# Score products in groups of four PSUM banks, a finer list schedule, and four smaller reorderings in an attention, expert and MLP kernel

## The chip, the cores and the metric

The kernel runs on one core of a Trainium2 chip. The metric is the device time of one execution in microseconds (us), smaller is better; a kernel's time is the median of several executions. The engines are PE (matrix products), DVE and ACT (elementwise work and copies out of PSUM), POOL (indirect gathers and scatters, some copies) and SP, whose queue issues most of the DMAs. PSUM has eight banks; PE writes its products there, and DVE and ACT read them out.

## The reference

Three layers in a row, in float32.

```
# 1 attention with mixing of the 12 heads before and after the softmax; q, k, v: 4 x 12 x 448 x 64
s = scale * q @ k^T;   s = einsum('bhij,hg->bgij', s, w_pre)
p = exp(s - max s);    p = p / (sum p + 1e-9)
p = einsum('bhij,hg->bgij', p, w_post);   x = p @ v        # then 1792 tokens x 768
# 2 one expert of 8 per token, chosen by argmax of x @ w_gate, weighted by its softmax
y = gate * (relu(x @ w1[e]) @ w2[e])                       # 768 -> 1024 -> 768
# 3 MLP
h = y @ w_in;  g = h * cos(h);  out = g @ w_out            # 768 -> 2048 -> 768
```

## The kernel before

**Products in three parts.** Most products are float32 split into a high and a low part (ACT makes the high part by a cast, DVE the low part by a subtraction), and three of the four partial products are added up in PSUM: high x high, high x low, low x high.

**Attention.** The work is 16 chunks: each of the 4 batches has three of 120 query rows and one of 88. For a chunk, `qk(X, j)` makes the scores of heads 2j and 2j+1 in two banks by six matmuls that use half of the array's rows each (the planner calls this tiling "row"). `brought` copies them to SBUF (tile S). A DMA from S to a tile x (`relay`) regroups them into blocks of up to 10 rows with their 12 heads on the partitions; there are 9 or 12 blocks to a chunk, 180 in all. A block is premixed (PE, m, line 515), reduced and exponentiated (DVE nm, ACT E), and mixed again (PE, pa, line 536) into AT. `products` multiplies a chunk's AT by v (PE, px, tiling "col"), and `gates` makes the router's logits of a few chunks.

**First batch.** The scores of chunk 0 are made by an order written out by hand, under `manual_schedule`: k and q of batch 0 arrive in pieces (`load_first`), POOL copies each pair of heads side by side (`beside`), PE transposes them (tp), ACT and DVE split them (KH, KL, QH, QL), and PE makes scores. `spin(n)` issues n products into a bank that nobody reads. `repeat` is a small product with w_pre and w_post; the mixing matrices `kpre` and `kpost` are made of its result by `mixers` at the end of this part.

**List schedule.** All other attention work is issued in an order that `Plan.run` finds when the program is built. Work is given as generators of steps; each step has a price per engine (time held, time until the result is there), PSUM banks and buffers to take and give back, and events to wait for. `Plan.run` takes the step that can start soonest, and among those within 0.02 us the one with the lowest rank, where a change of PE's tiling is charged `TURN` = 0.19 us and `LOYAL` is added to its rank. A DMA is a step on SP that holds SP 0.8 us and lands after a set time, whatever else is in flight. `score(X, j)` covers two calls of `qk` (four heads) as two steps of two banks each. `Banks` hands the planned banks to the tiles; outside the plan it takes the eight banks in turn. The plan begins where the first batch's part ends, with estimates of when each engine and bank is free; there every bank counts as free at time 0, from bank 0 on.

**From attention to the experts.** `between` runs the last chunk's products and logits among the first expert slot's first layer. `Routing.slots` makes the slot table, `slots_mm` turns it into row numbers (a product pid, then a copy to `ids` on DVE), and `Experts.lead` runs slot 0's second layer: `hT` transposes the hidden values and splits them (hh, hl), `product2` multiplies, and the token rows of slot 1 are gathered by POOL (`gather(1)`) after the first of the eight steps of `product2` and transposed (`xT(1)`, px, line 1174) after the sixth.

**MLP.** Four chunks of tokens (`CHUNKS`, 2, 4, 4 and 4 tiles of 128). `part2` adds, for each of 16 slices f of the hidden layer and each token tile, gh x oh, gh x ol and gl x oh into two banks: 512 columns in one, 256 in half of another. After f = 15 ACT copies the 512 columns, DVE the 256, and POOL scatters the rows to the output.

## Time and profile before

| | |
|---|---|
| median of 3 executions | 1329.72 us (1328.36 to 1333.59) |
| the profiled execution | 1326.42 us; span of its instructions 1324.7 us |
| busy share of the span | PE 98%, PE's weight loads 82%, DVE 79%, ACT 62%, POOL 5% |
| instructions | 24862 |
| attention, of that its first batch by hand | 0 to about 501 us, 0 to about 20 us |
| experts, with the way there from attention | about 501 to 843 us |
| MLP | about 833 us to the end (a little overlap) |

A row of a timeline gives start, duration, engine, source line, operation, the tiles written and read, and how many instructions were merged; in brackets stands the idle time of the engine before it and what ended it. A matmul's end is modelled and overlaps the next one's start, so distances between starts tell PE's pace better than durations do.

### The profile page before, as it was taken

The numbers are of one execution on the slowest core, as the hardware profiler recorded it, in microseconds if no ns is written. First come the engines' busy times: TensorE is split into PE (matmuls) and PEld (weight loads), VectorE is DVE, ScalarE is ACT, GpSimd is POOL, SyncE is SP. The second block draws the span as 40 slices with busy tenths as digits, with TensorE's granted clock in tenths as the row PEclk, the third lists the DMA queues.
The fourth block names the chain that finished last, engine by engine and source line by source line (L and its number), as shares of the span: only waits on it lengthen the run. The fifth ranks groups of instructions, "written<-read, shape, count | busy, mean of one in ns | idle before, by whom it ended". The sixth has DMA issues, their size and how long they took to land.

```text
span 1324.7 us, 24862 instructions
## 1 busy us (share of the span) xinstructions
PE 1300.1 (98%) x8855; PEld 1083.7 (82%) x8855; DVE 1042.6 (79%) x2410; ACT 824.0 (62%) x1509; POOL 67.8 (5%) x84
## 2 busy tenths in 40 slices
PE   8899999999999998999999999999999999999997
PEld 5677777677777777899999999998888888888886
DVE  7687888788778889899999999897666666666663
ACT  6566666566666657888889888765444444444432
POOL 3000000000000000100010000011000000001001
PEclk9999999999999999999999999999999999999999
DMA  6758757675757547278545772464433343224201
GB/s 162 229 192 228 228 169 223 203 235 172 218 188 220 175 153 247 87 270 319 185 167 190 286 266 93 147 225 168 152 101 115 108 132 109 85 96 142 94 25 48
DMA packets 146368, 227.02 MB, mean 171 GB/s; under 512 B 44800, under 2 KB 108480, under 8 KB 146240
## 3 DMA queue, kind: packets, MB, share of 16 engines
q1 hardware_dynamic: 139904, 200.20, 46.9%
q0 software_dynamic: 3744, 18.09, 4.0%
q10 hardware_dynamic: 2592, 7.08, 1.4%
q8 instruction: 73, 1.20, 0.4%
q14 instruction: 55, 0.45, 0.1%
HBM read 217.87 MB, written 31.85 MB: 189 GB/s over the span
## 4 chain that ended last, share of the span: by engine, by line
PE 59%; DVE 0%; ACT 0%; POOLq 0%; issue 0%
PE op L1466 18%; PE dh L1522 17%; PE yp L1280 11%; PE h L1246 11%; PE ph L1267 1%; PE px L1174 1%; PE dpt L1403 1%; POOLq L1769 0%; ACT dhs L1526 0%; ACT r L1489 0%; PE gspg L1023 0%; DVE r L1486 0%; DVE r L1487 0%; DVE o L1474 0%; PE pc L1059 0%
## 5 line engine op out<-in xcount | busy, mean ns | idle before, releaser
L1086 DVE TENSOR_TENSOR wl<-r,wh 128x768 fp32r<-128x768 f32 (+1 forms) x246 | 249.1, 1061 | 11.2 <-ACT wh L1085 8.3
L1085 ACT CAST wh<-r 128x768 fp32r<-128x768 f32 (+1 forms) x246 | 224.2, 931 | 37.9 <-PE h L1246 31.1
L536 PEld LDWEIGHTS pa<-kr,E 120*112 120x112 f32 (+1 forms) x1440 | 166.5, 177 | 45.6 <-issue 31.4
L536 PE MATMUL pa<-kr,E 120*112 120x120 f32 (+1 forms) x1440 | 180.7, 269 | 0.8 <-DVE kr L530 0.4
L1086 DVE TENSOR_TENSOR wil<-wi,wih 128x768 fp32r<-128x768 f32 x64 | 60.9, 953 | 131.3 <-ACT wih L1085 131.3
L515 PE MATMUL m<-x,kpre 120*120 120x448 f32 x360 | 159.8, 548 | 3.9 <-DMA x<-S 3.8
L522 ACT ACTIVATE E<-m,nm 120x448 f32<-120x448 f32 x180 | 114.5, 636 | 57.9 <-DVE nm L518 31.5
L1085 ACT CAST wih<-wi 128x768 fp32r<-128x768 f32 x64 | 53.9, 844 | 155.0 <-PE dh L1522 154.0
L518 DVE TENSOR_REDUCE nm<-m 120x1 f32<-120x448 f32 x180 | 111.2, 619 | 26.5 <-PE m L515 22.0
L1466 PE MATMUL op<-woh,gl 128*128 128x512 f32 x448 | 116.8, 341 | 0.0
L1466 PE MATMUL op<-woh,gh 128*128 128x512 f32 x448 | 116.0, 339 | 0.0
L1466 PE MATMUL op<-wol,gh 128*128 128x512 f32 x448 | 115.3, 338 | 0.0
L1522 PE MATMUL dh<-dxh,wih 128*128 128x512 f32 (+1 forms) x384 | 111.2, 364 | 0.1
L1522 PE MATMUL dh<-dxl,wih 128*128 128x512 f32 (+1 forms) x384 | 110.7, 363 | 0.0
L1522 PE MATMUL dh<-dxh,wil 128*128 128x512 f32 (+1 forms) x384 | 109.9, 363 | 0.0
L539 ACT COPY AT<-pa 112x480 f32<-112x480 f32 (+1 forms) x111 | 63.1, 568 | 43.8 <-PE pa L536 41.3
L1085 ACT CAST woh<-wo 128x768 fp32r<-128x768 f32 x64 | 53.4, 836 | 55.2 <-PE op L1466 54.6
L347 PEld LDWEIGHTS px<-AT,vn 112*64 112x64 f32 x1536 | 73.7, 137 | 10.2 <-issue 4.6
L1466 PEld LDWEIGHTS op<-woh,gh 128*128 128x128 f32 x448 | 70.7, 189 | 11.1 <-DVE o L1474 0.3
L1522 PEld LDWEIGHTS dh<-dxl,wih 128*128 128x128 f32 x384 | 70.1, 189 | 11.5
L1522 PEld LDWEIGHTS dh<-dxh,wil 128*128 128x128 f32 x384 | 69.8, 189 | 11.3
L515 PEld LDWEIGHTS m<-x,kpre 120*120 120x120 f32 x360 | 55.1, 183 | 28.9 <-issue 18.2
(290 smaller groups left out, 2561.1 us busy)
## 6 DMA issues: line engine op xcount, KB each, us to landing
r<-in_moe_w_dram SPq DMA_DIRECT2D x54, 1024.0 KB
r<-in_moe_w_dram SPq DMA_DIRECT2D x72, 768.0 KB
x<-S SPq DMA_DIRECT2D x172, 210.0 KB
wi<-wi SPq DMA_DIRECT2D x32, 768.0 KB
wo<-wo SPq DMA_DIRECT2D x32, 768.0 KB
W<-in_moe_w_in_dram SPq DMA_DIRECT2D x32, 384.0 KB
W<-in_moe_w_out_dram SPq DMA_DIRECT2D x32, 384.0 KB
ys<-y ACTq DMA_DIRECT2D x17, 384.0 KB
```

The source lines that it names most:

```text
L347: nc.tensor.matmul(px[64 * e : 64 * e + 64, pr, :n], VN[b, g // 3][:, g % 3, cc], AT[X][:, cc, g, :n], start=(cc == 0), stop=(cc == 3))
L515: nc.tensor.matmul(ps[:M, :S], kpre[:M, :M], x[:M], start=True, stop=True)
L518: nc.vector.reduce_max(nm[:M], ps[:M, :S], axis=AX.X, negate=True)
L522: last["act"] = nc.scalar.activation(e[:M], ps[:M, :S], AF.Exp, bias=nm[:M], scale=1.0, accum_out=sg[:M])
L536: nc.tensor.matmul(pa[:112, c, :120], e[:M, c * 112 : c * 112 + 112], kr[:M], start=True, stop=True)
L539: last["post"] = by[eng](AT[X][:, :, :, j0 : j0 + m], pa[:112, :, :120].rearrange("p c (g i) -> p c g i", i=10)[:, :, :, :m])
L1085: self.latest["A"] = nc.scalar.copy(hi, src).ins
L1086: self.latest["V"] = nc.vector.tensor_tensor(lo, src, hi.bitcast(F32), op=ALU.subtract).ins
L1246: self.nc.tensor.matmul(hp[n], a[:, k], w[:, n * 512 : n * 512 + 512], start=(k == 0 and i == 0), stop=(k == 5 and i == 2))
L1280: self.nc.tensor.matmul(yp[n][:, :384], a[:, k], w[:, n * 384 : n * 384 + 384], start=(k == 0 and i == 0), stop=(k == 7 and i == 2))
L1466: nc.tensor.matmul(bank[:, to], g[:, t * P : t * P + P], w[:, of], start=first, stop=(f == 15 and i == 2), skip_group_check=(n == 1))
L1522: nc.tensor.matmul(hp[:, :N], w[:, k], x[:, k, :N], start=(k == 0 and i == 0), stop=(k == 5 and i == 2))
```

## The change

It has these parts:

- `score` becomes one step for two calls of `qk`: it takes four banks at once, and its twelve matmuls follow each other. Scores get an earlier rank (n0 - 6 for n0 - 4), and `LOYAL` is 3 for 2.
- DMA steps carry what SP is held (0.34 to 1.36 us, by kind) and their size; the plan keeps a clock of the wire (260 KB per us) that all transfers share, and adds 0.6 us ahead and 1.97 us behind.
- The plan's starting state has its own times for each engine, bank and event. `Banks` keeps the banks in the order of their last use, and the plan starts from that order.
- First batch: the pieces of heads 4 to 7 are cut in two (two more DMAs each way are issued: one for k, one for q), `repeat` moves from the second to the fifth round, and two spins follow the second round's scores.
- `between`: the cast and subtraction of weight piece 4 (`ex.first(4)`) move behind the last chunk's logits and their copy.
- `lead`: `slots_mm` and `gather(1)` move from behind the first step of `product2` to between `hT`'s transposes and its splits.
- `part2`: the three 512-column products of a tile come first, then the three of 256 columns.

```diff
@@ -50,10 +50,13 @@
 
 
     def __init__(self, pool, n):
-        self.pool, self.given, self.turns = pool, [], itertools.cycle(range(n))
+        self.pool, self.given, self.turns = pool, [], list(range(n))
 
     def tile(self, shape, dt, tag, name):
-        i = self.given.pop(0) if self.given else next(self.turns)
+        i = self.given.pop(0) if self.given else self.turns[0]
+        if i in self.turns:
+            self.turns.remove(i)
+            self.turns.append(i)
         return self.pool.tile(shape, dt, tag=f"{tag}{i}", name=name)
 
 
@@ -66,12 +69,13 @@
 
 
 
-    HOP, TURN, STAY, LOYAL, DRIFT = 0.06, 0.19, 0.02, 2.0, 0.0
+    LEAD, LAND, RATE = 0.6, 1.97, 260.0
+    HOP, TURN, STAY, LOYAL, DRIFT = 0.06, 0.19, 0.02, 3, 0.0
 
     def __init__(self, slots, banks=None, seed=0):
         self.free = {t: [(0.0, i) for i in range(n)] for t, n in slots.items()}
         self.at, self.engine, self.pending, self.held = {}, {}, [], {}
-        self.now = self.reached = 0.0
+        self.now = self.reached = self.wire = 0.0
         self.tiling, self.banks, self.luck = "full", banks, random.Random(seed)
 
     def add(self, rank, task, bg=False):
@@ -141,6 +145,9 @@
             self.now = start
             self.engine[e] = start + hold
             end = start + lat
+            if "kb" in step:
+                self.wire = max(self.wire, start + hold + self.LEAD) + step["kb"] / self.RATE
+                end = self.wire + self.LAND
             for a in step.get("give", ()):
                 tag, key = (a, id(task)) if isinstance(a, str) else a
                 s = self.held[tag, key if tag == "q" else 0].pop(0)
@@ -150,8 +157,7 @@
                 self.at[ev] = end
             self.go(rank, task, bg, start + hold if step.get("onward") else end + self.HOP, e, slots)
         if self.banks:
-            self.banks.given = []
-            self.banks.turns = itertools.cycle([s for t, s in self.free["q"]])
+            self.banks.given, self.banks.turns = [], [s for t, s in self.free["q"]]
 
 
 class Taken:
@@ -244,7 +250,7 @@
     def load_first(a, src, h0, h1, cs=slice(0, 4)):
         nc.sync.dma_start(out=a[:, h0:h1, cs], in_=src[0, h0:h1].rearrange("h (p c) d -> p h c d", c=4)[:, :, cs])
 
-    for h0, h1 in ((0, 2), (2, 4), (4, 8), (8, H)):
+    for h0, h1 in ((0, 2), (2, 4), (4, 6), (6, 8), (8, H)):
         load_first(fk, k, h0, h1)
         load_first(fq, q, h0, h1, slice(0, 2))
     load_first(fq, q, 0, 6, slice(2, 4))
@@ -465,10 +471,12 @@
                 pk, pq_ = turned(0, j, 0), turned(0, j, 1, first)
                 if j == 0:
                     spin(2)
-                if j == 1:
+                if j == 4:
                     repeat()
                 if j > 0:
                     ps = qk(0, j - 1)
+                if j == 1:
+                    spin(2)
                 split_k(0, j, pk)
                 split_q(0, j, pq_, first)
             else:
@@ -501,13 +509,13 @@
         return {"ACT": (0.05 + n * 0.00092, 0.12 + n * 0.00092), "DVE": (n * 0.00124, 0.07 + n * 0.00124)}
 
     def dma(d):
-        return {"SP": (0.8, d)}
+        return {"SP": (d, d)}
 
     plan = Plan({"q": 8, "x": 6, "E": 4, "kr": 4, "Sb": 1, "AT": 1, "W": 2, "sq": 2, "f": 2, "kn": 2, "qn": 2, "xr": 1, "xc": 4, "vn": 0}, pq, 0)
 
     def block(n):
         X, be, rs, m, M = geom(n)
-        yield dict(run=dma(4.2), take=["x"], on=[("S", X, h) for h in range(H)], ends=[("x", n)])
+        yield dict(run=dma(0.86), kb=18 * M // 10, take=["x"], on=[("S", X, h) for h in range(H)], ends=[("x", n)])
         relay(n)
         yield dict(run=pe(0.752), take=["q"], reached=n)
         x = XR.pop(n)
@@ -547,8 +555,9 @@
             on += [("x", k) for k in range(first_of[X - 2], end_of[X - 2] + 1)]
         if j:
             on.append(("s", X, j - 1))
-        for i in (j, j + 1):
-            yield dict(run=pe(0.61), tiling="row", onward=True, take=[("q", ("s", X, i, h)) for h in range(2)], on=on, ends=[("s", X, i)])
+        js = range(j, j + 2)
+        yield dict(run=pe(0.6 * len(js) + 0.01), tiling="row", take=[("q", ("s", X, i, h)) for i in js for h in range(2)], on=on, ends=[("s", X, i) for i in js])
+        for i in js:
             SC[X, i] = qk(X, i)
 
     def brought(X, j, i):
@@ -559,7 +568,7 @@
     def heads(b, j, s_):
 
         tag, src, t = (("kn", k, KN), ("qn", q, QN))[s_]
-        yield dict(run=dma(4.0), take=[tag])
+        yield dict(run=dma(1.36), kb=230, take=[tag])
         load_pair(b, j, sk.tile([112, 4, 2, D], F32, tag=tag, name=f"{tag}{b}_{j}", bufs=2), src, t)
         yield dict(run=pe(0.385), take=["q"], on=[("s", 4 * b - 1, j)])
         ps = turned(b, j, s_)
@@ -574,7 +583,7 @@
 
     def values(b):
         for g in range(4):
-            yield dict(run=dma(3.5), on=[("av", 4 * b - 1, 0), ("av", 4 * b - 1, 1)] if b else [("x", 3)], ends=[("V", b)] if g == 3 else [])
+            yield dict(run=dma(0.58), kb=344, on=[("av", 4 * b - 1, 0), ("av", 4 * b - 1, 1)] if b else [("x", 3)], ends=[("V", b)] if g == 3 else [])
             load_v(b, g)
 
     def products(X):
@@ -636,29 +645,31 @@
         yield dict(run={"none": (0.0, 0.0)}, on=[("xcs", G_[-1])], give=["xc"])
 
     def piece(i, load, square, bits, store):
-        yield dict(run=dma(6.0), take=["W"])
+        yield dict(run=dma(0.58), kb=393, take=["W"])
         load(i)
         yield dict(run=act(0.56), take=["sq"])
         square(i)
         for d, op in zip((0.36, 0.56, 0.56), bits(i)):
             yield dict(run=dve(d), take=["f"] if d == 0.36 else [], give=["W", "sq"] if False else [])
             op()
-        yield dict(run=dma(3.5), give=["W", "sq"])
+        yield dict(run=dma(0.42), kb=197, give=["W", "sq"])
         store(i)
         yield dict(run={"none": (0.0, 0.0)}, give=["f"])
 
     for h in range(H):
-        plan.at["S", 0, h] = 0.0
+        plan.at["S", 0, h] = 0.7
     for j in range(H // 2):
-        plan.at["K", 0, j] = plan.at["Q", 0, j] = 0.0
+        plan.at["K", 0, j] = 0.0
+        plan.at["Q", 0, j] = 1.4 + 0.4 * j
+    plan.free["q"] = [(max(0.0, 0.6 + 0.4 * (i - 1)) if i > 1 else 0.0, s) for i, s in enumerate(pq.turns)]
     plan.add(4, values(0))
-    plan.engine.update(ACT=1.0, DVE=1.0, PE=0.5, SP=0.0)
+    plan.engine.update(ACT=3.0, DVE=3.3, PE=2.2, SP=0.0)
     for n in range(N):
         plan.add(n, block(n))
     for X in range(1, len(chunks)):
         n0, nb0 = first_of[X], CH[chunks[X - 1][1]][2]
         for j in range(H // 2):
-            r = n0 - 4 - 8 * (X % 4 == 3) - (H - 2 - 2 * j) * (nb0 - 5) / H
+            r = n0 - 6 - 8 * (X % 4 == 3) - (H - 2 - 2 * j) * (nb0 - 5) / H
             if j % 2 == 0:
                 plan.add(r, score(X, j))
             for i in range(2):
@@ -1094,7 +1105,7 @@
             yield
 
 
-MID, XT1 = 1, 6
+XT1 = 6
 
 ORDER = [(0, 0), (0, 1), (1, 0), (1, 1), (2, 0), (2, 1)]
 
@@ -1257,14 +1268,19 @@
         self.X.pop(s)
         return self.relu(hp, self.wk.tile([P, 1024], F32, tag="hr", name=f"hr{s}", bufs=1))
 
-    def hT(self, s, hr):
+    def hT(self, s, hr, mid=None):
         nc, wk = self.nc, self.wk
         hh = wk.tile([P, 8, P], F32R, tag="hh", name=f"hh{s}", bufs=1)
         hl = wk.tile([P, 8, P], F32R, tag="hl", name=f"hl{s}", bufs=1)
+        ps = []
         for half in range(2):
             p = self.pt.tile([P, 512], F32, tag="t", name=f"ph{s}_{half}")
             for j in range(4):
                 nc.tensor.transpose(p[:, j * P : j * P + P], hr[:, (4 * half + j) * P : (4 * half + j + 1) * P], self.ident)
+            ps.append(p)
+        if mid:
+            mid()
+        for half, p in enumerate(ps):
             pv = p.rearrange("p (a t) -> p a t", a=4)
             k = slice(4 * half, 4 * half + 4)
             self.spw.latest["A"] = nc.scalar.copy(hh[:, k], pv).ins
@@ -1315,12 +1331,13 @@
 
     def lead(self, mid):
 
-        self.hT(0, self.hr0)
+        def slots():
+            self.ids = mid()
+            self.gather(1)
+
+        self.hT(0, self.hr0, slots)
         yp = self.yp0 = self.hidden2(0)
-        self.product2(0, range(MID), yp)
-        self.ids = mid()
-        self.gather(1)
-        self.product2(0, range(MID, XT1), yp)
+        self.product2(0, range(XT1), yp)
         for _ in range(XT1, 8):
             self.split()
         self.xT(1)
@@ -1459,8 +1476,8 @@
             ci, f, gh, gl, oh, ol, op = item
             t0, nt = CH[ci]
             for t in tiles or range(nt):
-                for i, (g, w) in enumerate(((gh, oh), (gh, ol), (gl, oh))):
-                    for n, (bank, to, of) in enumerate(spans(op, t)):
+                for n, (bank, to, of) in enumerate(spans(op, t)):
+                    for i, (g, w) in enumerate(((gh, oh), (gh, ol), (gl, oh))):
 
                         first = f == 0 and i == 0 and (n == 0 or t % 2 == 0)
                         nc.tensor.matmul(
@@ -1618,9 +1635,9 @@
         ex.product1(0, 0, hp)
         ex.early_parts()
         att.av_out(X, 1, px, A)
-        ex.first(4)
         pl = att.logits_mm((X,))
         att.logits_out((X,), pl, V)
+        ex.first(4)
         att.rows_out(X, 0, att.rows_mm(X, 0), A)
         att.logit_tiles(X)
         ro.last(ctx, att.pq, "q")

```

## Rows read from the trace of the kernel before

**Rows 1.** Stretches: window, length, busy us of PE, PEld, DVE, ACT, POOL, PEclk, DMA share, GB/s

```profile
30.00:60.00 30.00, 26.14 (x212) 18.76 (x212) 20.27 (x69) 17.12 (x42) 0.00 (x0) 1.00 0.86 255
60.00:120.00 60.00, 58.68 (x483) 44.91 (x480) 49.60 (x144) 40.21 (x98) 0.00 (x0) 1.00 0.66 198
```

**Rows 2.** Chain that ended last: start us, us, what; MLP

```profile
863.12 4.32 PE dh L1522 x36
...
881.60 4.51 PE dh L1522 x36
...
1159.27 8.19 PE dh L1522 x36
1167.45 8.47 PE op L1466 x48
```

**Rows 3.** Timeline of the first batch, one wait

```profile
9.04 0.35 PE L437 MATMUL wps<-wpp,rep 12*120 12x24 f32 x2 [1.12 <-DMA wpp<-in_w_post_dram]
```

**Rows 4.** Stretches of 2 us in the first batch

```profile
8.00:10.00 2.00, 0.96 (x8) 0.74 (x8) 0.57 (x2) 0.43 (x2) 0.87 (x2) 1.00 1.13 238
10.00:12.00 2.00, 2.00 (x15) 1.17 (x13) 0.78 (x3) 1.65 (x4) 1.35 (x4) 0.80 1.18 227
12.00:14.00 2.00, 2.00 (x12) 1.67 (x12) 1.54 (x4) 1.31 (x3) 1.61 (x4) 0.50 1.13 198
14.00:16.00 2.00, 2.00 (x16) 1.17 (x14) 0.49 (x2) 1.23 (x3) 1.89 (x6) 0.85 0.17 22
```

**Rows 5.** Timeline where the list schedule begins

```profile
19.86 1.88 DVE L235 TENSOR_TENSOR QL<-tp,QH 128x224 fp32r<-128x224 f32 x6 [0.15 <-ACT QH L234]
...
21.79 0.47 PE L284 MATMUL s<-KH,QH 64*120 64x448 f32 x2 [1.48 <-DVE QL L235]
...
25.53 1.47 SPq L194 DMA_DIRECT2D kn<-in_k_dram  x2
...
35.60 1.01 PE L515 MATMUL m<-x,kpre 120*120 120x448 f32 x2 [1.96 <-DMA x<-S]
```

**Rows 6.** Waits from 30 to 495 us: who waited for what, total us, times, longest

```profile
PE m L515 <- DMA x<-S: 3.8, 6, 2.0
PE tp L216 <- DMA kn<-in_k_dram: 3.6, 4, 1.2
```

**Rows 7.** Timeline of PE at one visit to the scores

```profile
61.11 0.37 PE L284 MATMUL s<-KL,QH 64*120 64x448 f32 x2
61.32 0.37 PE L284 MATMUL s<-KH,QL 64*120 64x448 f32 x2
61.62 1.07 PE L536 MATMUL pa<-kr,E 120*112 120x120 f32 x8
```

**Rows 8.** Group of one line, 25 to 500 us: busy us, mean ns, idle before

```profile
L557 ACT COPY S<-s 120x448 f32<-120x448 f32 (+1 forms) x115 | 56.0, 538 | 12.5 <-PE s L284 11.6
```

**Rows 9.** Timeline between attention and experts

```profile
506.38 3.48 DVE L1235 TENSOR_TENSOR wl<-r,wh 128x1024 fp32r<-128x1024 f32 x3
...
509.78 0.23 DVE L358 COPY LT<-pl 8x88 f32<-8x88 f32 x1
```

**Rows 10.** Timeline of slot 0's second layer

```profile
519.70 1.28 DVE L1271 TENSOR_TENSOR hl<-ph,hh 128x512 fp32r<-128x512 f32 x2
...
521.76 0.17 DVE L951 CAST ids<-pid 128x21 int32<-128x21 f32 x1
...
522.21 3.19 POOL L1166 DMA_INDIRECT xg<-xs,ids  x1 [36.20 <-DMA r<-in_moe_w_dram]
...
528.26 0.87 PE L1174 MATMUL px<-ident,xg 128*128 128x128 f32 x6 [1.84 <-DMA xg<-xs,ids]
...
529.36 1.02 DVE L1184 TENSOR_TENSOR xl<-px,xh 128x384 fp32r<-128x384 f32 x2 [0.28 <-ACT xh L1180]
```

**Rows 11.** Timeline of the end

```profile
1317.53 0.59 ACT L1473 COPY o<-op 128x512 f32<-128x512 f32 x1 [1.62 <-PE op L1466]
...
1318.84 0.97 POOL L1475 DMA_INDIRECT out_dram<-o,cout  x1 [0.79 <-ACT o L1473]
```

## The prediction, made before the changed kernel was run

> **What bounds the kernel now.** I read the stretches first: PE is busy in almost all of every later stretch, and between 30 and 60 us it falls behind: 26.1 of 30 us, against 58.7 of 60 just after [rows 1]. Then the chain that ended last: from the expert stage on it is PE products back to back, 8.19 us for 36 products of 512 columns, 8.47 us for 48 of 512 and 256 alternating [rows 2]. DVE and ACT are off that chain. So time can be won in three ways only: take waits of PE away, give PE fewer or cheaper products, or shorten the tail. The third reading was of PE's waits, and they sit in five places: the first batch, where PE waits and its clock drops [rows 3, 4]; the start of the list schedule [rows 5]; waits for regrouped scores (x) and for the next batch's k in attention [rows 6]; the hand-over to the experts [rows 9, 10]; and the end [rows 11]. The sum is made against the profiled execution, 1326.42 us (span 1324.7, so 1.7 us lie around it). That is 3.3 us under the median of the runs, 1329.72; I take the saving as the same and carry it to the median.
>
> **First batch: -1.8 us.** PE waits 1.12 us for w_post before the small product of `repeat`, with the first scores queued behind it [rows 3]. In the fifth round that matrix has long landed, so the move costs only the product (0.35 us), and its copy on DVE no longer holds up the splits behind it. PE was busy 0.96 of 2 us from 8 to 10, and then the granted clock is 0.80, 0.50 and 0.85 in the next three stretches, the lower level for part of them [rows 4]. PE was called busy all that time, so the price of the drop is 2 x (0.20 + 0.50 + 0.15) = 1.7 us of work done at half speed. The two spins go into PE's queue ahead of the third round's transposes; they hold PE some 0.6 us, hidden by the wait for that pair's pieces, which the smaller pieces shorten; uncovered they cost that 0.6. The two extra DMAs take SP about 0.5 us each, while the DMA engines are the limit up to 14 us (share 1.13 to 1.18) and free after it (0.17) [rows 4], so they delay nothing that sets the end. Bounds: if ACT's and POOL's copies set the pace, 0.5; if wait and clock both go, 1.12 + 1.7 = 2.8. I take 1.8, between, since ACT is busy 1.65 of 2 us in one of these stretches.
>
> **Start of the plan: -1.2 us.** The first planned scores start at 21.79, after a wait of 1.48 us for a QL [rows 5]. They need the first head pair's QL alone, ready some 0.3 us into the six (19.86 to 21.74). They wait for the last: the plan gives bank 0, and counting tiles through the first batch bank 0 is the last one used (33 tiles, eight banks). With banks in order of use the four-bank step needs two score copies and the first two QL, about 20.5 to 20.6. Bounds 0 (x then sets the start) to 1.48; I take 1.2.
>
> **DMA prices: -2.5 and -1.8 us.** The plan holds SP 0.8 us for a pair's k where the trace shows 1.47 us for its two issues [rows 5], so real transfers of x fall ever further behind the planned ones; PE then waits 1.96 us for one at 35.60. In all PE waits 3.8 us for x in six places, and 3.6 us for k in four places, at the batch changes [rows 6]. With held times and a shared wire in the plan these steps stand later in PE's order, and blocks of ready work fill in. The list remains greedy: it still issues k, v or weight pieces whenever SP is free. Bounds 0 and 3.8, and 0 and 3.6. I take two thirds of the first, whose cause is seen, and half of the second.
>
> **Visits to the scores: -0.7, and +1.0 for the banks.** A visit costs a change of tiling twice: from the last score product to the next postmix 0.30 us, where score products follow each other at 0.21 [rows 7], so 0.09, and by the estimate of the same on the way in, about 0.19 a visit. I counted 49 visits in PE's timeline, 27 of a single pair; 45 four-head steps allow at most 45, and where steps follow each other fewer. Saved: 4 x 0.19 = 0.8 at the least expected, less if LOYAL's merging of whole runs of steps is lost; 0.7. Against it stands the added wait. Four of eight banks must be free together; behind a waiting step stand the premixes and postmixes, on PE in order. One bank comes free with one copy, 0.54 us on ACT [rows 8]. If the plan's prices are right it places the step where the banks are free; I price it at 0.54 us in two places, +1.0. From both sides: 0, or 0.54 at each of 45 steps, 24 us (a rival below).
> A page speaks against this part: the Trainium skill, TensorEngine Tiling (Array Packing), Gotcha 1: PSUM Pressure, says that row tiling raises the pressure on PSUM, as each row tile needs a bank of its own. By that rule the price would lie nearer the upper bound; the trace does not contradict it, as DVE and ACT do have waits for scores but PE's listed waits are on DMAs.
>
> **Hand-over to the experts: -0.2 and -1.8 us.** The copy LT (0.23 us, at 509.78) stands on DVE right behind three weight subtractions of 1.16 us [rows 9]. The move puts one of them behind it, so PE gets the logits' transposes, and the first layer behind them, up to 1.1 us sooner; but the copy of the transposed logits then waits behind that subtraction, and DVE is nearly full here. Bounds 0 and 1.1; I take 0.2.
> The gather of slot 1 starts at 522.21, right after `ids` at 521.76, and PE waits 1.84 us for it at 528.26 [rows 10]; this puts 6.05 us from start to use, a span that I keep. After the change two small products stand ahead of the splits hl on PE, and `ids` ahead of hl on DVE: it can run when hl now starts, at 519.70, instead of 521.76, 2.06 us sooner; hl and the first products behind it slip by about 0.2. Nothing else is on POOL's queue, and the gather is moved past no load of SP's. PE's wait shrinks to nearly nothing, 1.84 - 0.05 = 1.8. What comes next is xl, which DVE ends at 530.38; slot 1's first layer begins at about 532.4 and needs xl only at its third product, so there is cover of about 2 us, and it is just used up. Bounds 1.0 to 2.0.
>
> **Wide products first: -1.5 us.** A 512 and a 256 in turn take 8.47/24 = 353 ns. Wide ones alone take 8.19/36 = 227.5, narrow ones alone 4.32/36 = 120 or 4.51/36 = 125 [rows 2]: 347.5 to 353. So mixing costs 0.4 to 5.4 ns a pair. There are 14 x 16 x 3 = 672 pairs; if the cost sits at the changes of width, the new order keeps one in three, and saves 448 x (0.4 to 5.4) = 0.2 to 2.4 us. I take 1.5, nearer the quieter stretch of narrow ones. gl is needed 0.25 us sooner in each tile; its maker runs a slice ahead, so this is free.
> The Trainium skill, TensorE: Matmul & The Clock Gate, section Wait — 56ns, not 53.3ns?, has each matmul cost its columns plus a fixed amount; then the order makes nothing, and this term is 0. The rows neither prove nor exclude it, as 125 gives nearly that.
>
> **Tail: -0.3 us.** ACT's copy of the last 512 columns takes 0.59 us, and the last scatter starts 0.7 us after it ends [rows 11]. Its bank is now complete three narrow products (0.37 us) sooner; DVE's copy, which is shorter, then decides. Bounds 0.1 and 0.37.
>
> **Sum.** -1.8 - 1.2 - 2.5 - 1.8 - 0.7 + 1.0 - 0.2 - 1.8 - 1.5 - 0.3 = -10.8 us: 1326.42 - 10.8 = 1315.6 for a profiled execution, 1329.72 - 10.8 = 1318.9, say 1319, as a median.
>
> **Rivals.**
> 1. The plan gives back what it wins: another greedy order has other waits, in other places, and the plan's four terms (-1.2 of the start excepted) come to 0. They are -2.5 - 1.8 - 0.7 + 1.0 = -4.0, so 1323. For it: the waits of rows 6 are few and scattered and any new order draws new ones. Against: the price of SP is off by a factor that the trace shows.
> 2. Slower: four banks at once are not free where the plan believes so. At 0.54 us for each of 45 steps the change costs 24 us in place of 1.0, 1319 + 23 = 1342. It decides for slower (above 1336.4) from 18.4/45 = 0.4 us a step. For it: copies of scores end late where DVE and ACT wait for PE [rows 8] and the page above. Against: PE's waits on banks are absent among the large ones of the trace before.
> 3. All DMA waits and the clock's drop go: 1.0 more in the first batch, 1.3 on x, 1.8 on k, 1.0 on banks, together 5.1: 1314; more, if the visits merge as well.
> 4. The order of the widths makes nothing, as the page has it: the forecast moves to 1320.5. It goes beside any of the others; I give it 4 in 10.
>
> **How the numbers follow.** Forecast 0.50, rival 1 0.25, rival 3 0.15, rival 2 0.10. A measurement tells about 0.5% from no change, 6.65 us: faster is below 1323.1, slower above 1336.4. Of the forecast nearly all (0.47) is faster, of rival 1 half (0.12), of rival 3 all: 0.74. Rival 2 gives slower 0.08 and 0.02 between. Same: 0.18. The range reaches from 1310 (every bound of waits at its better end) to 1327 (rival 1 with the low bounds of first batch and hand-over, 1329.72 - 2.7); outside are most of rival 2 and a little of both ends.
>
> **What would show it.** Right: the granted clock stays at 1.00 in the first 20 us; the first planned score starts under 0.5 us after the last transposes; waits of m for x and of tp for k halve; 45 visits or fewer; px of slot 1 starts without a wait, 2 us closer to hl; 48 products of `part2` take 8.40 us or less. Wrong: new waits of PE's weight loads on copies of S or AT around the scores, a first batch that ends no sooner because POOL's copies or landings set it, or a stall of DVE in slot 0's second layer that takes the gather's gain.

## The result, and the profile after

| | median us | lowest to highest, runs | ratio to before, 95% interval |
|---|---|---|---|
| before | 1329.53 | 1328.36 to 1333.85, 6 | |
| changed | 1314.22 | 1313.68 to 1316.48, 6 | 0.9891 [0.9874, 0.9908] |

The change makes the kernel 1.1% faster: by the ratio 14.5 us, between 12.2 and 16.8. The profiled execution took 1316.38 us (span 1314.5) for 1326.42 (1324.7), a difference of only 10.2: that of before lay 3.1 us under its median, that of after 2.2 over its own. The 10.2 us come from these stretches, each taken between two starts that both traces have:

| stretch | before | after | difference |
|---|---|---|---|
| start to first premix (m) | 25.59 | 23.76 | -1.83 |
| first m to last postmix (pa) | 475.23 | 468.75 | -6.48 |
| last pa to slot 0's second layer (yp) | 18.48 | 17.69 | -0.79 |
| first yp to slot 3's first layer | 41.42 | 41.97 | +0.55 |
| slot 3 to the MLP's first dh | 272.09 | 272.09 | 0 |
| first dh to the end of the last op | 484.80 | 483.13 | -1.67 |
| from there to the end | 7.1 | 7.1 | 0 |

**Attention.** The stretches of the changed kernel, in the columns of [rows 1], with one row for nearly all of the list schedule:

```profile
30.00:60.00 30.00, 27.50 (x196) 18.73 (x197) 22.87 (x71) 17.40 (x42) 0.00 (x0) 1.00 0.84 228
60.00:120.00 60.00, 60.00 (x528) 46.79 (x526) 51.06 (x152) 41.06 (x101) 0.00 (x0) 1.00 0.75 217
24.00:490.00 466.00, 460.82 (x4193) 352.81 (x4193) 384.75 (x1298) 291.24 (x714) 1.31 (x2) 1.00 0.69 205
```

The last row in the trace of before:

```profile
24.00:490.00 466.00, 457.25 (x4142) 346.73 (x4139) 375.54 (x1269) 294.77 (x717) 1.23 (x2) 1.00 0.66 204
```

PE is idle 5.18 of these 466 us, where it was 8.75, and does 51 more products in them. The waits of PE from 30 to 495 us in the changed kernel, as in [rows 6]:

```profile
PE m L523 <- DMA x<-S: 2.3, 5, 0.9
PE tp L222 <- DMA qn<-in_q_dram: 1.0, 1, 1.0
```

The waits for x fell from 3.8 to 2.3 us, those for k from 3.6 to none that is listed; one for q came in. The timeline of PE at a visit to the scores shows the grouped step: a switch still costs 0.30 us where the products follow each other at 0.20 to 0.21, as in [rows 7], but there are 42 visits for 49, and 40 of them take two pairs.

```profile
67.90 0.37 PE L290 MATMUL s<-KL,QH 64*88 64x448 f32 x2
68.11 0.37 PE L290 MATMUL s<-KH,QL 64*88 64x448 f32 x2
68.41 1.07 PE L544 MATMUL pa<-kr,E 120*112 120x120 f32 x8
```

**First batch and the plan's start.** Stretches of 2 us, as in [rows 4], then the timeline, as in [rows 5]:

```profile
8.00:10.00 2.00, 2.00 (x20) 1.28 (x16) 0.98 (x3) 1.80 (x5) 1.15 (x3) 1.00 1.14 245
10.00:12.00 2.00, 2.00 (x18) 1.25 (x15) 1.93 (x4) 1.59 (x5) 0.61 (x1) 1.00 1.19 224
12.00:14.00 2.00, 1.91 (x15) 1.19 (x14) 1.14 (x5) 1.54 (x4) 1.81 (x5) 1.00 1.10 181
14.00:16.00 2.00, 2.00 (x18) 1.34 (x16) 1.64 (x5) 1.74 (x4) 1.66 (x5) 1.00 0.05 9
```

```profile
17.43 1.88 DVE L241 TENSOR_TENSOR QL<-tp,QH 128x224 fp32r<-128x224 f32 x6 [0.15 <-ACT QH L240]
...
17.77 1.42 SPq L200 DMA_DIRECT2D kn<-in_k_dram  x2
17.82 0.47 PE L290 MATMUL s<-KH,QH 64*120 64x448 f32 x2
...
19.30 5.13 SPq L307 DMA_DIRECT2D x<-S  x6
...
23.76 1.50 PE L523 MATMUL m<-x,kpre 120*120 120x448 f32 x3 [2.08 <-DMA x<-S]
```

PE is busy in all but 0.09 us from 8 to 16 us and its granted clock stays at 1.00, the 2.4 GHz level, where it had been busy for 0.96 of the 2 us from 8 to 10 and the clock fell. The splits QL start 2.4 us sooner than in [rows 5], and the first planned scores start 0.4 us after the first of them, without a wait. But two loads of k now stand on SP's queue ahead of the first x, which is issued 1.5 us later than it could be, and PE waits 2.08 us for it.

**Hand-over.** The timeline, as in [rows 10]; SPq is SP's queue of DMAs, and L1699 the line of a branch of the program that all engines pass:

```profile
510.43 0.17 DVE L962 CAST ids<-pid 128x21 int32<-128x21 f32 x1
510.52 1.28 DVE L1287 TENSOR_TENSOR hl<-ph,hh 128x512 fp32r<-128x512 f32 x2
510.88 0.98 POOL L1177 DMA_INDIRECT xg<-xs,ids  x1 [38.82 <-DVE ids L962]
...
515.29 0.07 SPq L1165 DMA_DIRECT2D r<-in_moe_w_dram  x1
...
516.91 0.82 PE L1185 MATMUL px<-ident,xg 128*128 128x128 f32 x6
...
524.84 6.74 ACT L1096 CAST wh<-r 128x1024 fp32r<-128x1024 f32 x7 [4.50 <-SPq L1699]
525.45 7.47 SPq L1161 DMA_DIRECT2D r<-in_moe_w_dram  x5
...
532.12 1.14 PE L1279 MATMUL ph<-ident,hr 128*128 128x128 f32 x8 [1.67 <-ACT hr L1261]
```

The wait for the gather is gone, and slot 1's first layer starts 10.82 us after the first yp (521.02 - 510.20) for 13.12 before. Then ACT stands still for 4.50 us at the branch, the relu hr of slot 1 comes late behind its casts, and PE waits 1.67 us for it. Slot 3 starts no sooner after the first yp than before (41.97 us for 41.42).

**MLP and tail.** Pieces of the chain that ended last, as in [rows 2], and the last copies and scatter, as in [rows 11]:

```profile
854.48 4.32 PE dh L1539 x36
...
1265.79 8.18 PE dh L1539 x36
1273.97 8.38 PE op L1483 x48
```

```profile
1307.09 0.59 ACT L1490 COPY o<-op 128x512 f32<-128x512 f32 x1 [1.60 <-PE op L1483]
1307.43 0.42 DVE L1491 COPY o<-op 128x256 f32<-128x256 f32 x1 [1.76 <-PE op L1483]
1308.63 0.97 POOL L1492 DMA_INDIRECT out_dram<-o,cout  x1 [0.77 <-issue]
```

48 products take 8.38 us for 8.47. At the end ACT's copy now starts before DVE's, but DVE's copy of the narrow columns is as late as it was, and the last scatter starts 1.24 us after the last product (1.23 before).

### The profile page after: what moved, and what is told of

Read it like the earlier page. It is cut to its first block, busy times and chain, and to the rows that moved or that the text cites. A ratio compares the mean times of both kernels' runs of the same rounds, so it can differ in the third digit from the quotient of the medians.

```text
span 1314.5 us, 24861 instructions
## 1 busy us (share of the span) xinstructions
PE 1294.2 (98%) x8857; PEld 1083.5 (82%) x8857; DVE 1046.8 (80%) x2419; ACT 817.5 (62%) x1500; POOL 75.0 (6%) x84
## 4 chain that ended last, share of the span: by engine, by line
PE 59%; ACT 0%; DVE 0%; issue 0%; POOLq 0%; ACTq 0%
PE op L1483 18%; PE dh L1539 17%; PE yp L1296 11%; PE h L1257 10%; PE ph L1279 1%; PE px L1185 1%; PE dpt L1420 1%; ACT wh L1096 0%; DVE wl L1097 0%; POOLq L1786 0%; ACT dhs L1543 0%; ACT r L1506 0%; DVE xl L1195 0%; PE gspg L1034 0%; DVE r L1503 0%
## 5 line engine op out<-in xcount | busy, mean ns | idle before, releaser
L1483 PE MATMUL op<-woh,gh 128*128 128x512 f32 x448 | 152.2, 340 | 0.0
L1483 PE MATMUL op<-wol,gh 128*128 128x512 f32 x448 | 151.9, 339 | 0.0
L1483 PE MATMUL op<-woh,gl 128*128 128x512 f32 x448 | 150.5, 336 | 0.0
L1483 PEld LDWEIGHTS op<-woh,gh 128*128 128x128 f32 x448 | 84.7, 189 | 11.3 <-DVE o L1491 0.2
L1483 PEld LDWEIGHTS op<-wol,gh 128*128 128x128 f32 x448 | 84.6, 189 | 9.9
L1483 PEld LDWEIGHTS op<-woh,gl 128*128 128x128 f32 x448 | 84.2, 188 | 9.9
L547 ACT COPY AT<-pa 112x480 f32<-112x480 f32 (+1 forms) x105 | 59.6, 567 | 47.3 <-PE pa L544 42.7
```

The lines of the kernel that those rows point to most:

```text
L547: last["post"] = by[eng](AT[X][:, :, :, j0 : j0 + m], pa[:112, :, :120].rearrange("p c (g i) -> p c g i", i=10)[:, :, :, :m])
L1483: nc.tensor.matmul(bank[:, to], g[:, t * P : t * P + P], w[:, of], start=first, stop=(f == 15 and i == 2), skip_group_check=(n == 1))
```

## The experiments

Twelve kernels ran, in three groups, each beside runs of the kernel before (medians 1329.1, 1329.1 and 1330.8). Each takes the changed kernel and puts something back, or adds something.

| kernel | median us | ratio to before, 95% interval | first m to last pa | PE idle from 24 to 490 |
|---|---|---|---|---|
| changed | 1314.22 | 0.9891 [0.9874, 0.9908] | 468.8 | 5.2 |
| plan_old | 1325.42 | 0.9971 [0.9955, 0.9986] | 479.9 | 11.9 |
| two_banks | 1312.96 | 0.9874 [0.9855, 0.9893] | 468.5 | 4.8 |
| dma_old | 1317.71 | 0.9915 [0.9895, 0.9935] | 467.8 | 4.3 |
| rank_old | 1314.49 | 0.9885 [0.9869, 0.9902] | 466.3 | 3.6 |
| rank_alone | 1315.20 | 0.9885 [0.9870, 0.9900] | 471.4 | 7.0 |
| x_first | 1312.28 | 0.9877 [0.9856, 0.9897] | 468.2 | 2.6 |
| start_old | 1308.61 | 0.9844 [0.9823, 0.9865] | 463.6 | 2.1 |
| drift_no_spin | 1314.41 | 0.9881 [0.9865, 0.9898] | 466.5 | 2.5 |
| es_late | 1312.21 | 0.9868 [0.9850, 0.9886] | 471.8 | 6.4 |
| es_late_lead_old | 1316.18 | 0.9907 [0.9886, 0.9927] | 467.2 | 4.7 |
| widths_old | 1316.91 | 0.9911 [0.9889, 0.9932] | 466.6 | 3.7 |
| start_old_es_late | 1307.79 | 0.9830 [0.9817, 0.9844] | 463.8 | 2.3 |

The last two columns come from one execution each. Their scatter can be read here: the changed kernel, es_late, es_late_lead_old and widths_old have the same attention, and its stretch came out at 466.6 to 471.8 us. A difference of under some 5 us in one trace is therefore no reading of the plan; the medians and their intervals are.

Part of that scatter is the clock. In es_late the granted clock falls to 0.50, the 1.2 GHz level, for 3.41 us from 160.0, just after a wait of PE of 1.28 us, and score products follow each other at 0.37 us for 0.20: that costs up to 1.7 of its 471.8 us. The other three of the four have no such fall, and they lie within 2.1 us (466.6 to 468.8). The same fall of 3.41 us is in the traces of plan_old (from 240.5), dma_old (23.8), x_first (154.0) and drift_no_spin (24.0), and one of 6.83 us in rank_alone (34.3), each time in or just behind waits of PE; it is not in those of changed, two_banks, rank_old, start_old and start_old_es_late. Stretches in the columns of [rows 1], es_late and rank_alone:

```profile
160.00:163.40 3.40, 3.40 (x20) 2.71 (x17) 2.36 (x10) 1.48 (x4) 0.00 (x0) 0.50 0.68 207
34.40:41.00 6.60, 5.26 (x15) 3.54 (x16) 2.30 (x5) 1.27 (x3) 0.00 (x0) 0.50 0.91 223
```

The times of executions show it too: of the twelve that plan_old had, the three with a mean clock of 0.999 took 1323.2 to 1324.2 us, and the one with 0.993 took 1332.0. So a wait that goes can save more than its own length. How much of each gain below comes this way was not measured.

### The plan as a whole: plan_old

All of the plan goes back (steps of two banks, DMA prices, start, banks in turn, rank, `LOYAL`); first batch, gates, hand-over and MLP stay changed. Two of the lines:

```diff
-        yield dict(run=dma(0.86), kb=18 * M // 10, take=["x"], on=[("S", X, h) for h in range(H)], ends=[("x", n)])
+        yield dict(run=dma(4.2), take=["x"], on=[("S", X, h) for h in range(H)], ends=[("x", n)])
...
-            r = n0 - 6 - 8 * (X % 4 == 3) - (H - 2 - 2 * j) * (nb0 - 5) / H
+            r = n0 - 4 - 8 * (X % 4 == 3) - (H - 2 - 2 * j) * (nb0 - 5) / H
```

> The changed kernel with the whole list schedule of before (two banks a step, old DMA prices, old start state, old ranks, banks in turn), everything else new. The gap between the two profiles splits as 1.8 us up to the first premix, 6.5 us from there to the last postmix, 0.3 us in the hand-over and 1.7 us in the MLP. Theory: the plan makes the 6.5 us and most of the first 1.8; then this kernel takes 7 to 8 us more than the changed one, its last postmix starts 7 to 8 us later, and it makes about 49 visits to the scores. Rival: the earlier end of the first batch alone shifts all that follows, and any order would do; then it costs 2 us or less.

Measured: 1325.42, so the plan is worth 0.0080 of 1329, 10.6 us, and all else 3.9. Its stretches and waits, in the columns used above:

```profile
24.00:490.00 466.00, 454.09 (x4110) 344.50 (x4108) 372.83 (x1263) 292.20 (x711) 1.22 (x2) 1.00 0.67 203
```

```profile
PE tp L219 <- DMA kn<-in_k_dram: 4.7, 5, 1.4
PE m L520 <- DMA x<-S: 4.3, 5, 2.3
```

The first batch's end stays at 16.94 us, and the waits for k and x are those of the kernel before, a little longer.

### Four banks: two_banks

```diff
-        js = range(j, j + 2)
-        yield dict(run=pe(0.6 * len(js) + 0.01), tiling="row", take=[("q", ("s", X, i, h)) for i in js for h in range(2)], on=on, ends=[("s", X, i) for i in js])
-        for i in js:
+        for i in (j, j + 1):
+            yield dict(run=pe(0.61), tiling="row", onward=True, take=[("q", ("s", X, i, h)) for h in range(2)], on=on, ends=[("s", X, i)])
             SC[X, i] = qk(X, i)
```

> The changed kernel with score steps of two banks each, as before; prices, start state and ranks new. Theory: four banks at once save visits only (41 in place of 49, about 0.19 us each), so this one takes about 1.5 us more and shows more than 45 visits. Rival: the four-bank step is what makes the attention stage 6.5 us shorter, then it takes 5 us or more in addition. Other rival: the wait for four free banks costs time; then this one is faster.

Measured: 49 visits for 42, and a median that is not above that of the changed kernel (0.9874 and 0.9891, the intervals overlap). Beside the new start, visits and bank waits together are worth nothing that can be measured.

### Which part of the plan: dma_old, rank_old, rank_alone

dma_old puts the DMA prices back, rank_old the rank and `LOYAL`. rank_alone is plan_old with these two as changed:

```diff
-    HOP, TURN, STAY, LOYAL, DRIFT = 0.06, 0.19, 0.02, 2.0, 0.0
+    HOP, TURN, STAY, LOYAL, DRIFT = 0.06, 0.19, 0.02, 3, 0.0
...
-            r = n0 - 4 - 8 * (X % 4 == 3) - (H - 2 - 2 * j) * (nb0 - 5) / H
+            r = n0 - 6 - 8 * (X % 4 == 3) - (H - 2 - 2 * j) * (nb0 - 5) / H
```

> Only the prices and sizes of the DMAs in the plan go back to those of before (SP held 0.8 us for each, a fixed time to land, no clock of the wire); four banks, the plan's start and all else stay as in the changed kernel. Theory A, the prices make most of the plan's gain (about 11 us in the median between the changed kernel and the one with the old plan): 5 to 9 us slower than the changed kernel, 1319 to 1323; PE waits for x and for k as in the kernel before (about 7 us in ten places from 30 to 490 us for 4 to 5 with the new prices). Rival B, the start makes most of it: under 3 us slower, at most 1317. Rival C, any order has its own luck and neither part alone carries the gain: both this kernel and the one with the old start lie near 1314, or both near 1325.

> Only the rank of the scores (n0 - 4 again) and LOYAL (2.0 again) go back in the plan; all prices, the start and the four banks stay as changed. All plans seen so far with the new rank end the last postmix at 487 to 496 us, whatever else was put back; the one with everything put back, the rank too, ends it at 502.7. Theory A, the rank carries most of the gain: last postmix at 499 us or later, 1321 to 1326 in the median, with more time of PE waiting for x or for regrouped scores. Rival B, the parts carry it together and any three hold it: last postmix at 496 or earlier, 1312 to 1318.

> The other way round: old DMA prices, old start, banks in turn, steps of two banks, and only the rank of the scores and LOYAL as in the changed kernel (first batch, hand-over and MLP as changed). Theory A, the rank carries the gain: last postmix at 487 to 496 us, 1310 to 1316 in the median. Rival B, the rank without the prices is worth little: 499 or later, 1321 to 1326.

Measured: taken from the changed kernel, neither part is clearly missed. Without the new prices the kernel is 0.0024 slower (3 us, intervals overlapping), without the new rank 0.0006 faster, as rank_old's rival had it. But rank and `LOYAL` alone, on top of the old plan, give 0.9971 - 0.9885, 11.4 us, the theory of rank_alone. So rank with `LOYAL` makes the whole gain by itself, and the other parts make it too when the rank is old.

Beside the new start, then, either will do, and the second adds nothing that is clear of noise. Beside the old start it is otherwise. rank_alone and start_old (below) both have the old start and the new rank, and differ by the DMA prices and the steps of four banks alone: 0.9885 [0.9870, 0.9900] and 0.9844 [0.9823, 0.9865], intervals apart. There these two parts add 0.0041, 5.4 us. So the medians add up as 11.4 us for the rank, 5.4 for prices and four banks behind it, and a loss of 6.2 by the new start, together the 10.6 of the plan. Prices and four banks were not taken apart on the old start. What the rank changes, in the waits of rank_alone:

```profile
PE m L520 <- DMA x<-S: 4.3, 2, 4.0
PE tp L219 <- DMA kn<-in_k_dram: 1.6, 3, 1.0
```

The 4.0 us for x is one wait, at 35.7 us: SP's queue has loads of k, q, v and weights from 23.5 to 28.8 ahead of the next x, as the old prices let it. Behind that the waits for x all but vanish (0.3 us), and those for k fall from 4.7 to 1.6. In the program the next batch's k is turned only once this batch's last scores are made, so earlier scores would bring earlier k; that is read from the program, and no run tries it. The slack of x doesn't settle it: from the issue of a block's x to its m there are 9.8 us in the median over 180 blocks in plan_old (9.6 before), and 11.0 in rank_alone, 10.7 in rank_old, 10.5 in the changed kernel, but 9.6 in drift_no_spin and 10.0 in start_old, which have the gain as well. PE's idle time explains 5 us of the 8.5 between the traces of plan_old and rank_alone; the rest lies inside what the profile counts as busy, and it isn't the clock, which was low for 3.41 us in plan_old and for 6.83 in rank_alone. So why the rank gains stays in part open, and rank and `LOYAL` were not taken apart.

### The plan's start: x_first, start_old

```diff
-        plan.at["S", 0, h] = 0.7
+        plan.at["S", 0, h] = 0.0
```

x_first has this line alone; start_old has the whole state of before, banks in turn too.

> The changed kernel, with the plan told that chunk 0's scores are there at its start (0.0 in place of 0.7 us). Theory: in the changed kernel SP issues the two pieces of k of batch 1 first, from 17.77 to 19.19, and the first x goes out at 19.30 though its scores were copied at 17.3; PE waits 2.08 us for it. With x first it goes out at about 17.4 and the first premix starts at about 21.9 in place of 23.76; if the later order is as good, the kernel is 1.5 to 2 us faster. Rival: the order changes as a whole and gives back what the start wins, between 2 us faster and 3 us slower, with the first premix still at 21.9.

> Only the state from which the plan starts goes back to that of before (all events and banks at 0, engines free at 1.0, 1.0 and 0.5, banks given in turn). Theory A (prices carry the gain): the first planned scores wait again for the last split, about 1.2 to 1.5 us, and that is the cost: 1315 to 1317. Rival B (the start carries it): 5 us or more slower, 1319 or above. A rival of its own: the old state has S ready at 0, so that x is issued ahead of k, as in the kernel in which only that time was put back; the first m would then start sooner (by up to 3 us) and outweigh the bank: 1312 to 1314.

Measured: x_first issues x ahead of k, and the first m starts 3.6 us sooner (timeline):

```profile
16.94 5.15 SPq L307 DMA_DIRECT2D x<-S  x6
...
20.13 0.98 PE L523 MATMUL m<-x,kpre 120*120 120x448 f32 x2
```

In the median that is 2 us, with overlapping intervals. start_old is faster by 0.0047, 5.6 to 6.2 us, more than any expectation had, and its interval lies clear of the changed kernel's. Its first scores do wait for the last split, as before (timeline), yet its first m starts at 23.76 us, like the changed kernel's, and the wait is more than made up: PE is idle 2.1 us from 24 to 490, less than half of the changed kernel's 5.2, with 1.5 us of waits for x.

```profile
17.95 3.52 SPq L304 DMA_DIRECT2D x<-S  x4
18.02 1.88 DVE L238 TENSOR_TENSOR QL<-tp,QH 128x224 fp32r<-128x224 f32 x6 [0.15 <-ACT QH L237]
19.66 0.76 PE L287 MATMUL s<-KH,QH 64*120 64x448 f32 x2 [1.18 <-DVE QL L238]
```

```profile
24.00:490.00 466.00, 463.89 (x4262) 357.91 (x4263) 392.59 (x1326) 290.63 (x711) 1.23 (x2) 1.00 0.69 210
```

The old start is the better one. The time at which S is ready explains the order on SP's queue; x_first's interval overlaps both, and which of the other values (engines, Q, banks) makes the rest stays open.

### Luck of the order, and the clock: drift_no_spin

```diff
-    HOP, TURN, STAY, LOYAL, DRIFT = 0.06, 0.19, 0.02, 3, 0.0
+    HOP, TURN, STAY, LOYAL, DRIFT = 0.06, 0.19, 0.02, 3, 0.5
...
-                if j == 1:
-                    spin(2)
```

> Two edits in stages that lie apart. In the plan every rank gets a random shift of up to 0.5 (DRIFT), so that another order comes out of the same prices; in the first batch the two spins behind the second round's scores are left out, the rest of that batch is as changed. Plan: if single orders scatter by chance as much as the parts of the change differ among themselves (487 to 496), the stretch from the first m to the last postmix lies 3 us or more away from the changed kernel's 464 to 472; if the rules decide and not the luck, inside it. First batch: if the spins hold the clock, the granted clock falls under 0.9 in some 2 us between 8 and 18 us and the last copy of the first scores ends 0.8 us or more later, at 18.3 or after; if the pieces and the moved small product did it, the clock stays at 1.00 and it ends at 16.9 to 17.9.

Measured, plan: 466.5 us from first m to last pa and 0.9881, inside the scatter of the changed kernel. One shuffled order under the same rules is as good, which speaks for the rules and against one lucky order. First batch: the clock stays at 1.00 without the two spins until 24.0 us, in the wait for the first x, and the last copy of the first scores ends at 17.67 us, among the 16.9 to 17.9 of the other runs (19.70 before). Two of the stretches:

```profile
8.00:10.00 2.00, 2.00 (x19) 1.38 (x17) 1.31 (x4) 1.48 (x4) 1.17 (x3) 1.00 1.14 228
10.00:12.00 2.00, 2.00 (x18) 1.44 (x18) 1.26 (x3) 2.00 (x6) 0.61 (x1) 1.00 1.19 232
```

The spins are not needed; the moved small product or the finer pieces keep PE busy here, which of the two was not tried.

### The hand-over: es_late, es_late_lead_old

The trace's records of SP show why ACT waits for SP's queue. Behind the load at 515.29 SP reads the expert numbers of later slots into registers, twelve reads one after another from 515.41 to 522.61, most of them 0.56 to 0.59 us apart, and only then comes to the branch that all engines pass. In the kernel before the same twelve ran from 524.67 to 531.9. After the first yp they end at 12.4 and 12.6 us: the reads did not move. Before, slot 1 started 13.12 us after the first yp and the reads were all but hidden (ACT waited 1.06 us); now it starts at 10.82. The 4.50 us are more than the reads: SP's first record behind its branch comes 1.65 us after the branch's, where it comes after 0.5 to 0.9 us in nine other traces that have the early gather and all the reads. In those ACT waits 3.3 to 3.7 us, and slot 3 starts 40.8 to 41.8 us after the first yp, about as before. es_late lets SP issue the loads of weights first:

```diff
-            e = self.nc.sync.value_load(src, min_val=0, max_val=E - 1)
+            with ExitStack() as c:
+                if 2 < s < NSURE:
+                    c.enter_context(self.tc.issue_after(self.spw.latest["S"]))
+                e = self.nc.sync.value_load(src, min_val=0, max_val=E - 1)
```

es_late_lead_old has this and, besides, the gather back behind the first step of the second layer:

```diff
-        self.hT(0, self.hr0, slots)
+        self.hT(0, self.hr0)
         yp = self.yp0 = self.hidden2(0)
-        self.product2(0, range(XT1), yp)
+        self.product2(0, range(1), yp)
+        self.ids = mid()
+        self.gather(1)
+        self.product2(0, range(1, XT1), yp)
```

> The changed kernel, but each slot's expert number is read into SP's registers behind the weight loads of the slot before, so that the twelve reads, 0.57 us each, no longer stand in SP's queue ahead of the branch. Theory: slot 1 starts 11.4 us sooner than in the kernel before and slot 3 only 8.5, since ACT waits 4.5 us for SP, which passes the branch late behind its register reads; without them this wait falls to below 1 us, the slots keep the lead, and the kernel is 2 to 3 us faster than the changed one. Rival: ACT waits for the weights, which land no sooner; then nothing is won (under 0.5 us) and the wait is for a DMA.

> The changed kernel with SP's register reads of slot 3 held back until the weights of that slot's time are issued (by itself 2 us faster than the changed kernel in the median, 2.9 in the trace from yp to slot 3), and now with the gather of slot 1 put back behind the first step of the second layer. If the early gather is worth its price once SP's reads no longer stand in the way: PE waits 1.5 to 2.2 us for xg again, and slot 1's first layer starts 1.8 us later after the first yp than with the early gather; 1314 in the median. If the time comes back at slot 2 or 3 in any case: slot 3 starts as long after the first yp as with the early gather, within 0.4 us, and the median stays at 1312.

Measured: in es_late one read stands before the branch, and ACT waits 0.73 us there; slot 3 starts 39.06 us after the first yp (41.97 in the changed kernel, 41.42 before). In the median that is 2 us, 1312.2 for 1314.2, with overlapping intervals. Timeline of SP's queue and ACT:

```profile
515.86 2.63 SPq L1168 DMA_DIRECT2D r<-in_moe_w_dram  x4
524.06 5.95 SPq L1164 DMA_DIRECT2D r<-in_moe_w_dram  x4
```

```profile
524.19 2.00 ACT L1096 CAST wh<-r 128x1024 fp32r<-128x1024 f32 x2 [0.73 <-PEq L1702]
```

With the old place of the gather on top, PE waits for it again (timeline) and slot 3 starts 41.48 us after the first yp:

```profile
517.11 0.87 PE L1188 MATMUL px<-ident,xg 128*128 128x128 f32 x6 [1.91 <-DMA xg<-xs,ids]
```

So in these traces the early gather is worth 2.4 us where SP's reads stand out of its way, and nothing clear where they don't. The medians go the same way (0.9868 and 0.9907), but their intervals touch.

The Trainium skill, DMA: Bandwidth & Descriptors, section Latency and other measured facts, gives about 600 ns as the floor of such a register read; the 0.56 to 0.59 us from one read to the next in this trace come close to it, of which the read's own record takes 0.26 to 0.28.

### The order of widths: widths_old

```diff
-                for n, (bank, to, of) in enumerate(spans(op, t)):
-                    for i, (g, w) in enumerate(((gh, oh), (gh, ol), (gl, oh))):
+                for i, (g, w) in enumerate(((gh, oh), (gh, ol), (gl, oh))):
+                    for n, (bank, to, of) in enumerate(spans(op, t)):
```

> Only the order of the products in the last matrix product goes back: 512 and 256 columns in turn. Theory A, each change of width costs some 2 to 3 ns: from the first dh to the end of the last op 1.0 to 1.7 us more, 48 products in 8.46 to 8.48 us for 8.38, 1315.5 in the median. Rival B, a fixed amount per product whatever its neighbour: 48 products in 8.38 us again, no difference in that stretch above 0.3 us. The tail in both: the end moves by no more than 0.1 us, since DVE's copy of the 256 columns starts after the last narrow product either way.

Measured: 484.79 us from the first dh to the end of the last op (483.13 changed, 484.80 before), and 48 products in 8.47 us again (chain that ended last, then the end of the timeline):

```profile
1247.47 8.17 PE dh L1539 x36
1255.64 8.47 PE op L1483 x48
```

```profile
1305.87 0.59 ACT L1490 COPY o<-op 128x512 f32<-128x512 f32 x1 [1.62 <-PE op L1483]
1305.99 0.42 DVE L1491 COPY o<-op 128x256 f32<-128x256 f32 x1 [1.78 <-PE op L1483]
1307.18 0.97 POOL L1492 DMA_INDIRECT out_dram<-o,cout  x1 [0.79 <-ACT o L1490]
```

The order is worth 1.66 us, and the tail nothing: the last scatter starts 1.23 us after the last product. With each change of width PE also changes the PSUM bank, and the two weights gh and gl follow each other in another order; no run separates these.

### Both improvements: start_old_es_late

The edits of start_old and es_late together.

> The two edits that have made the changed kernel faster, together: the plan starts from the state of before (x ahead of k on SP), and SP's register reads of slot 3 are held back. The stages lie apart, so the gains should add: 5.6 us of the one and 2.0 of the other in the median from 1314.2, so 1306 to 1308, and faster than both kernels. If the second is eaten at slot 3: 1308.5 to 1310.

Measured: 1307.79 us, 0.9830 [0.9817, 0.9844]: faster than the kernel before by 1.7% and than the changed one by 0.6%, the best version here. Slot 3 starts 39.92 us after the first yp for 41.47 in start_old, so the second gain is 1.6 us in the trace and 1.9 by the ratios, whose intervals overlap.

## Why the prediction was right, point by point

The forecast was 1319 with a range of 1310 to 1327; the median is 1314.2. Sign and cases were right, but the sum of -10.8 came from terms whose errors partly cancel, and that it came so near is in part luck: a gain of 11.4 us by the rank had no term, and against it stand a loss of 6.2 us by the start, forecast as a gain of 1.2, and a gather whose 1.8 us did not last. By the ratio the sum should have been -12.2 to -16.8. The lower end of the range, 1310, is a little further than the better bounds of all terms reach: they add up to 18.4 us, 1311.4.

- **First batch, -1.8.** Its last score copies end 1.8 to 2.8 us sooner over all runs, so the term lies at the low end of what was measured, and the upper bound of 2.8 was nearer. The cause was half right: wait and clock drop went together, but without need of the spins.
- **Start of the plan, -1.2.** Wrong in sign. The step was that sooner first scores bring a sooner first m. They did start sooner, but the new state also put two k loads ahead of x, and the plan from the old state is 5.6 to 6.2 us faster.
- **DMA prices, -2.5 and -1.8, visits and banks, -0.7 and +1.0.** Together with the start they were to give -5.2; the plan gave -10.6. The failing step is that the new rank had no term: it was read as a part of the visits, while it alone, with `LOYAL`, gives the whole gain. The waits named, x and k, were the right ones, and they fell from 7.4 to 2.3 us. The mechanism of the prices is not refuted: rank_old keeps the gain without the new rank, and behind the new rank the prices are worth 3 us by the medians with the new start, not clear of noise, and 5.4 together with the four banks on the old one, where -4.0 was forecast for these four terms. Visits fell further than forecast, to 42, and with the new start the two small terms came to nothing that can be measured.
- **Rival 1**, a plan that gives back what it wins, is refuted by plan_old, though the start alone does give back 6.2 us. **Rival 2**, banks at 0.54 us a step, by two_banks. **Rival 3** came nearest, by other causes: x still waits, k doesn't.
- **Gates, -0.2.** The stretch from the last pa to the first yp is 0.8 us shorter in the changed kernel's trace, within the term's bounds. It was not tried by itself, and in the other kernels, which all have this move, the stretch is 16.99 to 18.94 us for 18.48 before.
- **Gather, -1.8.** The wait of 1.84 us went, and slot 1 came 2.3 us sooner, more than forecast; xl, named as next, held nothing up. What was missed is the next step behind it: SP's register reads end when they ended, and the time is given back at slot 3. "Moved past no load of SP's" was true and beside the point: reads are no loads. The stall it named as a sign of being wrong is there in seven of the twelve traces with the early gather, as a wait of PE for hl of 0.75 to 0.78 us, but slot 1 starts hardly later after the last pa in them (28.6 to 29.1 us, for 28.5 to 30.3 in the other five and 31.6 before).
- **Widths, -1.5.** Right, 1.66 measured. **Rival 4**, the order makes nothing, is refuted: 8.47 and 8.38 us are the same 48 products. 32 of 48 changes of width are saved there for 0.09 us, 2.8 ns each; over the whole MLP 896 changes are saved for 1.66 us, 1.9 ns each, so the price is not the same everywhere. A fixed amount for each product, as the Trainium skill has it (TensorE: Matmul & The Clock Gate, section Wait — 56ns, not 53.3ns?), would have given the same time for both orders.
- **Tail, -0.3.** Zero. The sentence that DVE's copy then decides was the answer: it starts behind the last narrow product in either order.

## What to carry to other kernels

In a greedy schedule, price each parameter by itself, ranks above all, and put each back alone and all together: two remedies for one wait can each look worthless when the other is there, and a third part that costs time can hide what one of them gives. When a wait is removed, follow every engine up to the next point that all of them pass, with register reads and branches, which the tables of busy time leave out. A start state that is truer for one engine can be worse for the queue behind it, so look at what it issues first.

## What the runs showed of the hardware

- 24 products of 512 columns and 24 of 256 take 8.47 us when width and PSUM bank change at each, and 8.38 when they change at every third.
- Twelve register reads on SP take 7.2 us, while that queue issues nothing; ACT waits 3.3 to 3.7 us at the branch behind them in nine traces, and 4.50 in one where SP's first record behind the branch comes late.
- In seven of the fourteen traces the granted clock falls to the 1.2 GHz level once before the end, for 3.41 or 6.83 us, in or just behind waits of PE (1.28 us in es_late, 3.96 in rank_alone). The changed kernel's wait of 2.08 us at the first x went by without a fall, while drift_no_spin's of 2.06 had one.
- Executions of one attention program differ by up to 5 us between first m and last pa (466.6 to 471.8), by 2.1 us where the clock never fell.
